# A chunked attention in one form for all blocks, with wide loads for the first six head pairs and W's first words ahead of block 1's loads

## The chip, the cores and the metric

The kernel runs on one core of one Trainium2 chip. The metric is the device time of one execution in microseconds. A core has TensorE (PE, with PEld for its weight loads), VectorE (DVE), ScalarE (ACT), GpSimd (POOL) and SyncE (SP). Loads and stores are issued from the queue of SP, POOL or ACT, and 16 DMA engines carry them.

## The reference

Three steps follow each other. First an attention in chunks: 4 batches, 8 heads, 768 tokens, heads of 64. A chunk of 32 tokens sees 16 tokens to its left, itself, 8 to its right, and 8 memory keys.

```python
for c in range(nc):
    l_start, r_end = max(0, c_start - left_ctx), min(S, c_end + right_ctx)
    k_full = np.concatenate([mem_k, k[:, :, l_start:r_end]], axis=2)
    v_full = np.concatenate([mem_v, v[:, :, l_start:r_end]], axis=2)
    scores = scale * np.matmul(q_c, k_full.transpose(0, 1, 3, 2))
    a = np.exp(scores - max); a = a / (sum(a) + 1e-09)
    out[:, :, c_start:c_end] = np.matmul(a, v_full)
```

Then two layers on the 3072 tokens by 512 columns: `g = h * tanh(softplus(h))` with `h = x @ w_in`, `x = g @ w_out` (hidden width 2048), and the same with `g = h * sigmoid(1.702 h)`. The four weights come as float64.

## The kernel before

The tokens go in 8 blocks (j) of 384. For each block the attention leaves x in a tile `xh` (and its low word in `xl`), and `forward(j, f)` multiplies it by 128 columns of w_in, for 16 f's (L1218). Block 0 does so in plain f32 (4 matmuls of 384 columns an f), blocks 1 to 7 as three products of a high and a low word (12 matmuls). Behind the first layer's forwards `across` and then `first` and `second` do the rest in products that are not touched here.

A float64 weight arrives as pairs of 32-bit words in `wi0` to `wi15`, and ACT and DVE make an f32 of it in `wo0` to `wo15` (`w_conv`: the drop L416 or L419, the shift L425, the low word L429, the sign L433). `split_words` then cuts it into two words for blocks 1 to 7 (L529, L534).

The attention stands in two forms. Blocks 0 and 1 use quads: the rows of all heads are loaded as they lie (`rows_of_heads`), turned on PE (`turned`, L761), multiplied four at a time (L829, L789), masked and reduced on DVE (`least`, L845), normed (L880), turned (L911, L991), multiplied with v (L928, L1013). Block 1's quads lie between block 0's forwards. Blocks 2 to 7 use duos of two head pairs: q and k are loaded in pieces of 32 columns (128 bytes), turned by DVE in 32 x 32 squares (L669, L672), the chunks' scores go to PE (L1054, 48 small matmuls, 96 instructions), then the maxima (L1069), exp (ACT, L1076), norm (L1088), three transposes a head (L1096), and the product with v (L1116, as many).

Every operation is handed to a planner (`Plan.add`) with a rank, costs for each engine that may do it, and the tiles that it reads and writes; `Plan.issue` writes each engine's order from these. The engines go through their own order one by one and wait where a tile isn't ready. A `Tag` is a set of buffers; the next user waits for the last one of the same buffer.

Of the kernel before, what the change touches and what calls it, by code (L numbers as in the profile page):

```python
# [9 lines left out]
F32 = mybir.dt.float32  # L10
# [8 lines left out]
EARLY = 2  # L19
WARM = 16  # L20
LEAD = 8
SOON = 12
AHEAD = 6
# [3 lines left out]
STAGGER = 1.5  # L27
LATE = 3
TURN = 2.7
# [70 lines left out]
class Spread:  # L100

    def __init__(self, before, *places):
        self.before, self.places, self.bufs = before, places, len(places)
        self.made = []
# [8 lines left out]
class Part:  # L113
# [9 lines left out]
    def __getitem__(self, key):  # L123
        return self.get()[key]

# [5 lines left out]
class Plan:  # L131
# [12 lines left out]
    def add(self, rank, ways, reads=(), writes=(), updates=(), chain=None, table=None):  # L144
# [5 lines left out]
        op.after, op.at = [], 0.0  # L150
        need = {}
# [7 lines left out]
        for b in (*writes, *updates):  # L159
# [3 lines left out]
            if not b.users and b.tag is not None:  # L163
                if b.inside is not None and b.inside.tag.made[0] is not b.inside:
                    below = b.inside.tag.made
                    k = below.index(b.inside)
                    b.gate += [(o, True) for o in below[k - b.inside.tag.bufs].users]
                    below[k - b.inside.tag.bufs].closed = True
                made = b.tag.made
                k = made.index(b)  # L170
                if isinstance(b.tag, Spread) and k < b.tag.bufs:
                    b.gate += [(o, True) for o in b.tag.before.get(b.inside, ())]
# [127 lines left out]
def bus(nbytes, run):  # L300
    return nbytes / 290e3 * (1 if run >= 512 else 1.3 if run >= 256 else 1.8)
# [3 lines left out]
def kernel(  # L305
# [24 lines left out]
    GQ = 96  # L330
    NG = S // GQ
    GB = TB // GQ
    WIN = P - NM
# [8 lines left out]
    NQ = H // 2 * (GB // 2)  # L342
    HV = H // 2
# [20 lines left out]
    T.update(ql=Shared(z0, 0), kl=Shared(z0, TB), mem_t=Shared(z0, TB + 32 * NKB), qT=Shared(z1, 0), kT=Shared(z1, 448))  # L364
    T.update(gh=Shared(z2, 0, TB), aT=Shared(z3, 0, TB))
    T.update(tags(ps, h=2, s0=1, s1=1, **{f"o{i}": 1 for i in range(4)}))
    for f in range(NF):
        T.update(tags(sb, **{f"{n}{f}": 1 for n in ("wi", "wo")}))

    def load(rank, buf, parts, nbytes, run, reads=(), early=False, via=None):  # L370

        for part in parts:
            def go(queue, part=part):
# [3 lines left out]
            size = bus(nbytes / len(parts), run)  # L377
            ways = [
                ("sp", 0.475, lambda go=go: go(nc.sync), size),
                ("pool", 1.2, lambda go=go: go(nc.gpsimd), size),  # L380
            ]
            add(rank, [("pool", 0.8, *ways[1][2:])] if via else ways if early else ways[:1], reads=reads, writes=[buf])
# [61 lines left out]
    def w_first(f):  # L444
        if f % 2 == 0:
            pairs.append(T[f"wo{f // 2}"].new([P, 2 * DM], F32))
# [1276 lines left out]
```

## Time and profile before

| | us |
|---|---|
| median of 3 runs (lowest, highest) | 1103.59 (1102.69, 1104.82) |
| the profiled execution | 1105.13 |
| its span | 1103.3 |
| busy in the span: PE, PEld | 1079.3, 1041.1 |
| busy in the span: DVE, ACT, POOL | 800.3, 555.8, 98.6 |

The profiled execution's own time is 1.8 us longer than its span, the part of the execution that lies around the profiled instructions. The shares of busy time are means over stages that are not alike: the start, in which loads and attention come first, block 0's forwards with block 1's attention between them, blocks 1 to 7, and the rest. The table of stretches below cuts there.

### The profile page before, as it was taken

How to read it: one execution, taken by the hardware profiler on the slowest of the kernel's cores; microseconds unless marked ns; L12 is line 12 of the kernel's file. 1: busy time of each engine (PE TensorE's matmuls, PEld its weight loads, DVE VectorE, ACT ScalarE, POOL GpSimd, SP SyncE). 2: the span in 40 equal slices, each digit the busy share in tenths (PEclk: the TensorE clock that was granted, in tenths of full speed). 3: DMA queues.
4: the chain of work that ended last, by engine and by line, in shares of the span. 5: the costliest groups of instructions: out<-in, count | busy, mean ns of one | idle time of the engine just before them, and what ended most of it. 6: DMA issues, size and time to landing. Idle time of an engine off the chain costs nothing.

```text
span 1103.3 us, 24808 instructions
## 1 busy us (share of the span) xinstructions
PE 1079.3 (98%) x9642; PEld 1041.1 (94%) x9642; DVE 800.3 (73%) x1456; ACT 555.8 (50%) x1246; POOL 98.6 (9%) x169
## 2 busy tenths in 40 slices
PE   7899999999999999999999999999999999999998
PEld 6568898989999999999999999999999999999998
DVE  5997656756556688899879856666657787877875
ACT  5875453545454455555455565555555533333332
POOL 2005642432300000000000000000000000000000
PEclk9999999999999999999999999999999999999999
DMA  9988998899986854663552686868688536345361
GB/s 172 264 241 189 242 247 228 205 250 268 278 276 222 249 175 147 216 212 121 189 172 86 208 260 223 296 227 290 203 265 261 160 106 166 112 133 145 105 165 46
DMA packets 278733, 221.28 MB, mean 201 GB/s; under 512 B 113553, under 2 KB 253868, under 8 KB 278616
## 3 DMA queue, kind: packets, MB, share of 16 engines
q1 hardware_dynamic: 272055, 209.46, 64.9%
q0 software_dynamic: 6560, 10.24, 3.8%
q8 instruction: 76, 1.25, 0.5%
q14 instruction: 42, 0.34, 0.1%
HBM read 138.33 MB, written 81.26 MB: 199 GB/s over the span
## 4 chain that ended last, share of the span: by engine, by line
PE 78%; DMA 10%; DVE 5%; SPq 4%; issue 1%; ACT 1%; DVEq 0%; ACTq 0%
PE o L1481 9%; PE o L1573 9%; PE h L1218 9%; PE o L1218 8%; PE h L1380 7%; PE o L1380 6%; PE s L1481 6%; PE h L1573 6%; PE h L1481 6%; PE s L1573 5%; SPq L375 4%; PE s L1380 3%; DMA st<-wd 3%; DMA st<-in_moe_w_out_dram 2%; DMA g1d<-ev 1%
## 5 line engine op out<-in xcount | busy, mean ns | idle before, releaser
L1218 PE MATMUL h<-xh,wi 128*128 128x384 f32 x320 | 82.9, 340 | 0.0
L1218 PE MATMUL o<-xh,wi 128*128 128x384 f32 x320 | 82.7, 339 | 0.0
L1218 PEld LDWEIGHTS h<-xh,wi 128*128 128x128 f32 x320 | 57.2, 188 | 0.6
L1218 PEld LDWEIGHTS o<-xh,wi 128*128 128x128 f32 x320 | 57.0, 188 | 0.5
L1218 PE MATMUL h<-xl,wi 128*128 128x384 f32 x160 | 53.7, 336 | 0.0
L1218 PE MATMUL o<-xl,wi 128*128 128x384 f32 x160 | 53.7, 336 | 0.0
L1350 ACT ACTIVATE e<-h 128x384 f32<-128x384 f32 (+2 forms) x47 | 22.4, 477 | 45.4 <-PE h L1573 28.8
L1573 PE MATMUL o<-wo,xh 128*128 128x256 f32 x232 | 43.7, 282 | 0.0
L1563 DVE TENSOR_TENSOR xl<-vt,xh 128x1024 fp32r<-128x1024 f32 x24 | 29.3, 1223 | 19.7 <-ACT xh L1560 18.0
L1563 DVE TENSOR_TENSOR xl<-wi,xh 128x1024 fp32r<-128x1024 f32 x32 | 38.8, 1222 | 5.9 <-ACT xh L1560 5.1
L1481 PE MATMUL o<-xh,wo 128*128 128x256 f32 x224 | 40.5, 282 | 0.0
L1560 ACT ACTIVATE xh<-wi 128x1024 fp32r<-128x1024 f32 x25 | 26.4, 1056 | 23.0 <-DMA wi<-gd 12.4
L375 POOL DMA_DIRECT2D vt<-in_v_dram x50 | 32.2, 648 | 63.3 <-PE o L1116 33.6
L375 POOL DMA_DIRECT2D wo<-in_v_dram x50 | 31.7, 638 | 53.7 <-PE o L1116 51.1
L1464 DVE TENSOR_TENSOR xl<-z,xh 128x1024 fp32r<-128x1024 f32 x24 | 29.2, 1222 | 9.7 <-ACT xh L1460 9.1
L1218 PE MATMUL o<-wo,wi 128*128 128x384 f32 x192 | 36.2, 340 | 0.0
L1573 PEld LDWEIGHTS o<-wo,xh 128*128 128x128 f32 x232 | 36.0, 190 | 0.0
L1218 PE MATMUL h<-wo,wi 128*128 128x384 f32 x192 | 35.7, 339 | 0.0
L1481 PEld LDWEIGHTS o<-xh,wo 128*128 128x128 f32 x224 | 34.6, 190 | 0.0
L1218 PEld LDWEIGHTS h<-wo,wi 128*128 128x128 f32 x192 | 33.2, 188 | 0.2
L1218 PEld LDWEIGHTS o<-wo,wi 128*128 128x128 f32 x192 | 33.0, 188 | 0.4
L1350 ACT ACTIVATE ev<-o 128x384 f32<-128x384 f32 (+2 forms) x31 | 14.5, 469 | 36.7 <-PE o L1573 17.5
(460 smaller groups left out, 3499.6 us busy)
## 6 DMA issues: line engine op xcount, KB each, us to landing
st<-in_moe_w_out_dram SPq DMA_DIRECT2D x32, 512.0 KB
st<-wd SPq DMA_DIRECT2D x29, 512.0 KB
z<-g1d SPq DMA_DIRECT2D x24, 512.0 KB
vt<-gd SPq DMA_DIRECT2D x24, 512.0 KB
wi<-gd SPq DMA_DIRECT2D x24, 512.0 KB
g1d<-gl SPq DMA_DIRECT2D x46, 192.0 KB
g1d<-z SPq DMA_DIRECT2D x45, 192.0 KB
wi<-in_moe_w_in_dram SPq DMA_DIRECT2D x16, 512.0 KB
```

What stands on the lines that cost most here:

```text
L375: queue.dma_start(out=o, in_=i)
L1218: nc.tensor.matmul(out=h.get(), lhsT=a[:, c], rhs=b.at(kk), start=(n == 0), stop=(n == KD * len(prods) - 1))
L1350: ("act", act(n, True), lambda: nc.scalar.activation(out=dst(), in_=bank.get(), func=AF.Copy)),
L1380: nc.tensor.matmul(out=bank.get(), lhsT=a, rhs=b, start=(fresh and m == 0), stop=(m == 3 * K2 - 1), skip_group_check=not fresh,)
L1464: add(rank + 0.05, [("dve", dve(n2), lambda gh=gh, gl=gl, src=src: nc.vector.tensor_tensor(out=flat(gl), in0=flat(src), in1=flat(gh), op=A ...
L1481: nc.tensor.matmul(out=bank[:, d, :], lhsT=a, rhs=b[:, p, :], start=(fresh and h == d == p == m == 0), stop=(h == 1 and p == HP - 1 and m ...
L1560: ("act", act(NP * P), lambda: nc.scalar.activation(out=flat(gh), in_=flat(src), func=AF.Copy)),
L1563: add(rank + 0.05, [("dve", dve(NP * P), lambda: nc.vector.tensor_tensor(out=flat(gl), in0=flat(src), in1=flat(gh), op=ALU.subtract))], re ...
L1573: nc.tensor.matmul(out=bank.get(), lhsT=a[:, p], rhs=b, start=(fresh and p == 0 and m == 0), stop=(p == NP - 1 and m == 2), skip_group_che ...
```

## The change

The quads go, with their masks, and all blocks use duos. `wide_pair` is new: for block 0's four head pairs and block 1's first two, q and k come in 1-KB pieces (4 tokens of a head in one partition), PE turns them by eight plain matmuls with the unit matrix (`turn`, L681), and ACT or DVE copies the result out in token order (L695, L696). The other pairs keep the 128-byte pieces. Block 0's q loads are issued by ACT; later blocks' q loads move from SP's queue to POOL's; all of v's come on POOL's. The memory rows of v are loaded for even blocks alone and stay in the tile for the odd ones. W's first words (for block 0) come in 2-KB pieces, two f's at a time and half of the 512 rows each, so that an f needs two tiles (`Joined`), and the ranks (LEAD is -2) place block 1's loads behind the first five of them. Block 0's h has three eviction buffers in place of two, and the planner's costs for a load (`bus`) are other ones.

The first forward in PE's order, before (L1218; `xh_312` is block 0's x, `wo0_469` the first W tile, `o1_551` and `ev_438` are block 0's scores and weights of a quad):

```order
L789 MATMUL o0_549<-z1_152 96x128
L789 MATMUL o1_551<-z1_152 96x128
L911 MATMUL o2_572<-ident_64,ev_438 128x96 x4
L928 MATMUL o3_585<-z3_267,vt_128 64x96 x4
L1218 MATMUL h_600<-xh_312,wo0_469 128x384 x4
L991 MATMUL s0_625<-ident_64,e_523 128x96 x4
L1218 MATMUL h_633<-xh_312,wo0_469 128x384 x4
L991 MATMUL s1_658<-ident_64,e_563 128x96 x4
L1218 MATMUL o2_663<-xh_312,wo1_544 128x384 x4
```

and after (L901 is the forward; `wo11_670` and `z1_80` are block 1's keys and queries of the second duo, `e_664` the weights of its first):

```order
L850 MATMUL s1_718<-z3_439,vt_315 64x32
L850 MATMUL o1_720<-z3_439,vt_315 64x32
L788 MATMUL s0_780<-wo11_670 32x64
L788 MATMUL o0_782<-wo11_670 32x64
L788 MATMUL s0_780<-z1_80 32x64
L788 MATMUL o0_782<-z1_80 32x64
L830 MATMUL s1_838<-ident_64,e_664 128x128 x3
L901 MATMUL h_845<-xh_635,wo0_313 128x384 x4
L901 MATMUL h_868<-xh_635,wo0_313 128x384 x4
L830 MATMUL o1_900<-ident_64,e_680 128x128 x3
L901 MATMUL o2_906<-xh_635,wo1_422 128x384 x4
L850 MATMUL s1_949<-z3_439,wo12_104 64x32
```

Before, the last product with v of block 0 (L928) stands just ahead of the first forward, and block 1's quads follow between the forwards. Now 48 scores matmuls of block 1's second duo and a group of transposes of its first stand ahead of it; rows that only repeat are left out.

DVE's order ahead of the first forward, before (`wo0_469` is a W tile in conversion, `e_563` and `mx_564` belong to block 1's quads):

```order
L918 COPY z3_267<-o2_513 128x384
L806 RECIPROCAL r_518<-r_518 96x4
L845 ISA e_523,mx_524<-s1_493,mask_70 96x128
L880 TENSOR_TENSOR ev_438<-ev_438,r_518 96x512
L965 COPY xh_312<-o3_539 128x192
L845 ISA e_563,mx_564<-s0_491,mask_70 96x128
L845 ISA e_563,mx_564<-s1_493,mask_70 96x128
L425 TENSOR_SCALAR wo0_469<-wo0_469 128x512
L425 TENSOR_SCALAR wo1_544<-wo1_544 128x512
```

and after (`z1_80` is the tile of queries and keys on which the scores above wait):

```order
L730 STREAM_TRANSPOSE wo11_670<-z0_194 128x384
L447 SCALAR_TENSOR_TENSOR wo2_488<-wi5_170,wo2_488 128x512
L733 STREAM_TRANSPOSE wo11_670<-z0_194 128x13x32
L730 STREAM_TRANSPOSE z1_80<-wo13_293 128x384
L646 COPY wo11_670<-z0_194 128x12x8
L433 TENSOR_SCALAR wo3_692<-wi6_323 128x512
L439 TENSOR_SCALAR wo3_692<-wo3_692 128x512
L555 TENSOR_TENSOR wi1_698<-wo0_313,wi0_515 128x512
L822 TENSOR_TENSOR e_680<-e_680,r_709 128x384
L733 STREAM_TRANSPOSE z1_80<-wo13_293 128x13x32
L443 SCALAR_TENSOR_TENSOR wo3_692<-wi6_323,wo3_692 128x512
L646 COPY z1_80<-z0_194 128x12x8
```

The maxima with mask (L845) are gone from there. W's conversion (L433, L439, L443, L447) now lies between the transposes of block 1's queries and keys (L730, L733), and the copy of the memory keys into `z1_80` (L646) closes them.

SP's queue at the start, after:

```order
L388 DMA wi12_92<-in_k_dram 100x2x256
L388 DMA wi13_96<-in_k_dram 100x2x256
L631 DMA wo12_104<-in_mem_k_dram 8x4x32 x4
L388 DMA wi14_98<-in_k_dram 100x2x256
L388 DMA wi15_102<-in_k_dram 100x2x256
L388 DMA wi0_136<-in_moe_w_in_dram 128x2x512
L388 DMA wi1_139<-in_moe_w_in_dram 128x2x512
L388 DMA wi2_142<-in_moe_w_in_dram 128x2x512
L388 DMA wi3_145<-in_moe_w_in_dram 128x2x512
L388 DMA wi4_155<-in_moe_w_in_dram 128x2x512
L388 DMA wi12_92<-in_q_dram 96x2x256
L388 DMA wi5_170<-in_moe_w_in_dram 128x2x512
```

k of block 0 comes first there, then five W tiles in 2-KB pieces (`128x2x512`), then block 1's first q; before, the queue began with block 0's k, q and v in pieces of 256 bytes.

```diff
@@ constants
-LEAD = 8
+FIRST = 4
+WIDE = 2
+LEAD = -2
@@ tags
+    T["ql"] = Spread((z0, 0), (w13, 0))
+    T["kl"] = Spread((z0, TB), (w13, TB))
+    T["qT"] = Spread(*((z, 0) for z in (z1, w15, w11)))
+    T["kT"] = Spread(*((z, TB) for z in (z1, w15, w11)))
+    T["vh"] = Spread(*((z, 0) for z in (w12, w14, *vs)))
...
@@ load
-            add(rank, [("pool", 0.8, *ways[1][2:])] if via else ways if early else ways[:1], reads=reads, writes=[buf])
+            way = ("sp", 0.475, lambda go=go: go(nc.sync), bus(nbytes / len(parts), run))
+            if on == "act":
+                way = ("act", 0.5, lambda go=go: go(nc.scalar), way[3])
+            elif via:
+                way = ("pool", via, lambda go=go: go(nc.gpsimd), bus(nbytes / len(parts), run, True))
...
@@ w_conv, w_first
+            k, c = (KD, 2 * P) if half is None else (KD // 2, 4 * P)
...
+        whole = T[f"wo{f // 2}"].new([P, 2 * DM], F32)
+        halves = [Part(whole, i * DM, DM) for i in range(2)]
+        for i in range(2):
+            w_conv(1, f, 0, f - 1.5, (), halves[i], f"wi{f + i}", i)
+            wi[f + i] = (Joined(halves, i),)
...
+    def wide_pair(j, hp, rank):
+        n, few = 4, LEFT // 4
+        nq, nk = TB // n, NKB * CHUNK // n
...
+        load(rank - lead, ql, [lambda: (
+            ql[:nq].rearrange("p h r d -> p h (r d)"), rows(q, r0, [(n, nq), (S, 2)], 0, n * D)
+        )], 2 * TB * D * 4, 1024, on=None if j else "act")
...
+        def turn(raw, m, t):
+            for r in range(n):
+                for hh in range(2):
+                    nc.tensor.matmul(
+                        out=t[hh * D:(hh + 1) * D, r * m:(r + 1) * m], lhsT=raw[:m, hh, r], rhs=ident[:m, :m],
+                        start=True, stop=True, tile_position=(0, hh * D),
+                    )
...
@@ pair_of_heads
+        if j == 0 or j == 1 and hp < WIDE:
+            return wide_pair(j, hp, rank)
...
-        load(rank - 4, ql, qs, P * TB * 4, 128)
-        load(rank - 4, kl, ks, P * NKB * 128, 128)
+        load(rank - (LEAD if j == 1 else 4), ql, qs, P * TB * 4, 128, via=NARROW * (j > 1))
+        load(rank - (LEAD if j == 1 else 4), kl, ks, P * NKB * 128, 128)
...
@@ values_of
+            if s0 == 0:
+                parts.append(lambda row=i * D + CHUNK, h=h: (
...
@@ forward
-        if j == 0:
-            w_cut(f)
-        t = T[("gh", "gl", "ev")[i % 3] if j else ("gh", "gl")[f % 2]].new([P, TB], F32)
+        if j == 0 and f % 2:
+            w_cut(f - 1)
+        t = T[("gh", "gl", "ev")[i % 3]].new([P, TB], F32)
```

## Rows read from the trace of the kernel before

**Rows 1.** Stretches of the span: start:end, length, busy us (instructions) of PE, PEld, DVE, ACT, POOL, clock, DMA, GB/s
```profile
0.00:39.07 39.07, 28.50 (x272) 23.67 (x272) 24.79 (x134) 24.71 (x99) 5.94 (x14) 0.96 1.01 201
39.07:94.20 55.13, 53.78 (x370) 33.40 (x369) 51.59 (x150) 39.51 (x124) 3.57 (x7) 1.00 0.88 230
94.20:380.00 285.80, 280.40 (x3634) 270.41 (x3633) 175.02 (x435) 139.39 (x468) 89.05 (x149) 1.00 0.89 245
```

**Rows 2.** Timeline of PE from 39 us: start us, us, engine, line
```profile
39.07 2.85 PE L1218 MATMUL h<-xh,wo 128*128 128x384 f32 x8
```

**Rows 3.** Stretches of 1 us at the start, columns as in rows 1
```profile
14.00:15.00 1.00, 0.00 (x0) 0.00 (x0) 1.00 (x11) 0.00 (x0) 0.00 (x0) 1.00 1.29 174
18.00:19.00 1.00, 1.00 (x8) 0.96 (x6) 0.00 (x0) 0.91 (x3) 0.00 (x0) 0.50 1.11 211
21.00:22.00 1.00, 1.00 (x12) 0.73 (x8) 1.00 (x7) 0.31 (x2) 0.00 (x0) 1.00 1.15 240
```

**Rows 4.** Chain of waits, 0 to 62 us: start us, us, what
```profile
45.57 5.19 PE o L1218 x16
50.76 0.41 PE h L761 x4
```

**Rows 5.** Groups of PE's instructions from 39.07 to 94.2 us
```profile
L991 PE MATMUL s<-ident,e 96*128 96x96 f32 x16 | 1.9, 249 | 0.2 <-DVE e L880 0.2
L1013 PE MATMUL s<-z,vt 128*64 128x96 f32 x32 | 1.8, 252 | 0.0
...
L761 PE MATMUL h<-ident,wi 96*128 96x96 f32 x8 | 1.7, 254 | 0.0
...
L789 PE MATMUL s<-u 64*96 64x128 f32 x16 | 1.1, 279 | 0.0
```

**Rows 6.** Chain of waits, 60 to 112 us
```profile
73.44 1.05 PE o L789 x16
...
86.71 0.66 PE o L991 x8
...
89.98 0.17 PE s L1054
...
91.08 0.81 PE o L1013 x16
...
99.27 0.48 PE o L1096 x3
...
108.09 0.17 PE s L1116
...
109.63 1.25 PE h L1218 x6
```

**Rows 7.** Timeline of DVE, 58 to 61 and 91.5 to 96 us
```profile
58.85 0.43 DVE L425 TENSOR_SCALAR wo<-wo 128x512 int32<-128x512 int32 x1 [0.36 <-ACT wo L416]
59.20 0.68 DVE L433 SCALAR_TENSOR_TENSOR wo<-wi,wo 128x512 int32<-128x512 int32 x1
59.80 0.68 DVE L429 SCALAR_TENSOR_TENSOR wo<-wi,wo 128x512 int32<-128x512 int32 x1
...
92.36 0.54 DVE L1069 TENSOR_REDUCE mx<-o 128x6 f32<-128x384 f32 x1
92.82 0.33 DVE L1071 TENSOR_SCALAR mx<-mx 128x6 f32<-128x6 f32 x1
92.88 0.60 DVE L672 STREAM_TRANSPOSE z<-wo 128x416 f32<-128x416 f32 x1
```

**Rows 8.** Timeline of PE at the start
```profile
1.36 6.67 PE L1631 MATMUL o<-ident 128*128 128x128 f32 x32 [1.36 <-POOL ident masks.py:199]
```

**Rows 9.** Waits of PE, 95 to 240 us: in total, times, longest
```profile
PE s L1096 <- DVE e L1088: 1.5, 1, 1.5
```

**Rows 10.** The page's costliest groups, POOL's loads of v
```profile
L375 POOL DMA_DIRECT2D vt<-in_v_dram x50 | 32.2, 648 | 63.3 <-PE o L1116 33.6
```

**Rows 11.** DMA issues: out<-in, queue, count, KB each, median us to landing
```profile
wi<-in_q_dram POOLq DMA_DIRECT2D x1, 192.0 KB, 8.9
```

## What the change is predicted to do

> **What bounds the kernel now.** I read the table of the stretches first, because the change acts on the start alone and a mean over the span hides it. The program's first matmul of the first layer (L1218, block 0) starts at 39.07 us [rows 2]; I call this moment T0. Before T0 PE works 28.50 of 39.07 us; behind it PE works 53.78 of 55.13 us, then 280.40 of 285.80, and DVE has room in both (51.59 of 55.13, 175.02 of 285.80) [rows 1]. The reader is to see two regimes: a start in which PE waits for others, and a rest in which PE is the bound. So the time is T0, plus the PE work that stands behind T0, plus the little PE idles there. The chain of waits says what a piece of that work takes: 16 matmuls of L1218 take 5.19 us, and 8 of them are one f of block 0 [rows 4], so block 0's sixteen take 8 x 5.19 = 41.5 us. The rest of the stretch 39.07 to 94.20 is block 1's attention, which lies between block 0's matmuls.
>
> The clock view shows a loss inside the start: PE does nothing from 14 to 15 us (it waits there for q and k), the clock is then granted at 0.50, and is at 1.00 again from 21 us [rows 3]. Half of the some 3.5 us between is lost, 1.75 us.
>
> **The change part by part.** *T0.* In the new order PE's first L901 is queued behind the scores of block 1's second duo, and their last operand is a key tile that DVE turns (L733) and completes (L646). So T0 hangs on DVE's order up to that copy. Counted there from block 0's first maxima: 13 W operations of the low and sign kind and 2 of the low-word kind at 0.60 us (59.20 to 59.80), 7 shifts and 2 drops at 0.35 (58.85 to 59.20), 21 operations of about 384 columns (6 maxima, 6 norms, 5 copies out of PSUM, 4 transposes) at 0.46 (92.36 to 92.82), 27 small ones at 0.1, where the one measured took 0.06 (92.82 to 92.88) [rows 7]. That is 9.0 + 3.15 + 9.7 + 2.7 = 24.5 us. It begins when block 0's first scores stand: the warm-up matmuls end at 8.03 [rows 8], six turnings (L681) behind them go in q, k pairs. A turning is 16 PE passes over 96 to 104 columns; the trace has none of it, so by its nearest rows: not under 0.41 us (L761's four, [rows 4]), not over 1.34 (L789's 1.05 for 16 of 128 columns [rows 6], with the quarter added that serial passes would cost); I take 0.85, near to L1013's 0.81 for 16 [rows 6]. 8.0 + 6 x 0.85 = 13.1, one duo's scores 1.1 (89.98 to 91.08 [rows 6]): 14.3. 14.3 + 24.5 + 0.6 for one stall at the first W word = 39.4; behind it half of the scores (0.6) and three transposes (0.48 [rows 6]). T0 = 40.5, 1.4 later than now. Ends: 37.5, where small operations go at 0.06 and ACT takes copies that I counted on DVE; 45, in the rival below.
>
> *What stands behind T0.* Before, block 1's attention still has there, by the groups of PE [rows 5] (each has a twin of the same count, o beside s, or wo beside wi) and their time in the chain: 32 of L991 at 0.66 for 8, 2.6; 64 of L1013 at 0.81 for 16, 3.2; 32 of L789 at 1.05 for 16, 2.1; 16 of L761 at 0.41 for 4, 1.6 [rows 4, 6]. Together 9.5 us. After, of block 1 there remain three transposes at 0.48 and two products with v at 1.54 (108.09 to 109.63 [rows 6]): 4.5. Saved: 5.0. The maxima with mask (L845) go from DVE and come back as plain maxima; both lie beside PE's work behind T0 and count nothing there. If DVE's room there were gone, its idle 3.5 us of that stretch [rows 1] would be the price.
>
> *Idle of that stretch.* 55.13 less 41.5, 9.5 and 1.1 (scores of block 2) is 3.0. It stems from PE pieces that wait for DVE or ACT between f's; with fewer pieces I keep half: -1.5. Bounds -3 and +1.5, by all of it going or half as much coming.
>
> *The clock at T0.* In the new order PE's work on attention before T0 lies in short pieces with waits for DVE, in the last of them some 5 us long. The only such wait in the trace, 13.7 to 17.2, is followed by 0.50 for some 3.5 us [rows 3]. I put one such dip at T0 and none at the start (block 0's q now comes from ACT's queue in 1-KB pieces, the warm-up runs straight into it): 1.75 now and inside T0, 1.75 then, partly behind T0. The one inside T0 is gone from the chain that I worked out afresh, so I charge +1.7. Bounds 0 and 6 (two more dips plus every small PE piece of the chain at half speed).
>
> The Trainium skill, "TensorE: Matmul & The Clock Gate", Part 1 on the HAM clock gate, says that the throttled state is the default and that activity releases it. The rows agree with the direction: 0.50 stands behind an idle stretch [rows 3]. It speaks against this change, whose start leaves PE sparse for longer; by it the clock would be low in the whole of 14 to 40 us, which is the first rival.
>
> *Queues.* Block 0's four q loads go to ACT, later blocks' q from SP to POOL. POOL's operation for v takes 0.648 us and the 50 of this group wait 63.3 us, most for PE's product [rows 10]; so a q load can stand behind a v load that waits. I cost it at -0.5 (SP is relieved of four issues a pair, odd blocks of eight memory loads). PE's longest wait between 95 and 240 us is 1.5 us [rows 9]; bounds -3 and +3, two of that size gone or come. The 2-KB pieces of W halve the number of pieces; W's tiles are not the last to come by the sum above, so that counts nothing; if they were, the price would be in T0 and within its bounds.
>
> *Sum:* +1.4 - 5.0 - 1.5 + 1.7 - 0.5 = -3.9. The profiled execution took 1105.13 us (span 1103.3 and 1.8 around it), 1.54 over the median 1103.59. 1105.13 - 3.9 = 1101.2, so a median of 1099.7 us. This case alone: 1096.5 to 1102.5, by the terms' bounds taken two at a time.
>
> **The rivals.**
> *A cold, late start.* From the first scores on PE is busy in pieces of 0.5 to 1.5 us with waits between; if 0.50 is granted all through, turnings, scores and transposes on the chain to T0 take twice as long: two more turnings and a scores group are 2 x 0.85 + 1.1 = 2.8 on it, and the copies wait with them. For: 18 to 21 us [rows 3]. Against: the mean clock of the whole start is 0.96 today, with PE at work in 28.50 of 39.07 us [rows 1]. T0 = 43.5 to 45, +3.5 on the sum: about 1103.3, no change.
> *More than forecast.* All idles of the stretch go, no dip, DVE's chain starts a turning earlier, T0 as now: -5.0 - 3.0 - 1 = -9, so about 1094.5. For: PE is the bound for the rest, and each us before it counts in full. Against: DVE's 24.5 us are in order.
> *Slower: POOL's queue holds q.* The stretch of blocks 1 to 7's first layer has two duos a block, one in 285.8 / 14 = 20.4 us [rows 1]. In a duo POOL issues 8 v and 8 q loads, 16 x 0.648 = 10.4 us; the v loads wait for the product of a duo before. What a q load then still needs is its landing and the DVE turning. The one q load of POOL in the trace took 8.9 us to land [rows 11]. 10.4 + 8.9 = 19.3, 1.1 under the period; with a landing over 10.0 us PE would wait. A landing 1 us over that would cost 1 us in each of the 12 duos of blocks 2 to 7: about 1111.7. For: 1.1 us is little. Against: that load moved 192.0 KB, and a q load of the new order moves 48 (32 partitions of 12 x 32 words).
> *It doesn't do what it says.* W's first words, issued earlier, might not land earlier, since W and block 0's loads share the DMA engines; T0 hangs on DVE's order all the same, so the sum stays, and its chance is part of the forecast's.
>
> **How the numbers follow.** Forecast 0.52, more than forecast 0.15, the cold start 0.20, POOL's queue 0.13. A measurement here can tell about 0.2% from no change, 1101.4 and 1105.8. Faster holds 0.40 of the forecast's 0.52, the 0.15, and 0.05 of the cold start: 0.60. Same holds 0.12 of the forecast and 0.12 of the cold start: 0.24. Slower: 0.03 of the cold start and all of POOL's: 0.16. The range 1093 to 1107 leaves out half of POOL's case and the end of "more": under 2 in 10.
>
> **What would show it.** T0 between 39.5 and 42 in the timeline of PE, with the scores of block 1's second duo just ahead of it; three L830 and two L850 groups of block 1 behind it; the first forward of block 1 some 49 us behind T0 (41.5 + 4.5 + 1.1 + 1.5 = 48.6, before 55.1). It is wrong if T0 is over 44, if the clock is at 0.50 behind 45 us, if PE waits between 95 and 380 us for keys or queries by more than 5 us in sum, or if PE's idles of block 0 stay at 3 us.

## The result and the profile after

The changed kernel takes 1112.51 us (median of 4 runs, 1112.08 to 1116.74), the kernel before 1103.38 beside it (4 runs, 1102.69 to 1104.82). The ratio is 1.009, interval 1.0063 to 1.0116. It is slower by 9.1 us; 3.9 less was predicted. The profiled execution took 1112.08 us. Ratios here and below are of fast executions; of all runs one execution, of e8_before_q_on_pool (3523.88 us), was slow.

The page after: busy us, share of the span and instructions, and the granted clock in 40 slices.

```profile
PE 1080.3 (97%) x10242; PEld 1046.0 (94%) x10242; DVE 790.4 (71%) x1342; ACT 536.1 (48%) x1183; POOL 167.5 (15%) x280
...
PEclk7699999999999999999999999999999999999999
```

PE is as busy as before (1080.3 against 1079.3), so 7 us more of span are not more work. The second and first slices show a lower clock.

The stretches after, columns as in [rows 1], cut at the first matmul of the first layer (T0), up to the first forward of block 1.

```profile
0.00:55.38 55.38, 35.19 (x816) 31.34 (x817) 30.22 (x86) 26.61 (x101) 25.29 (x48) 0.71 0.95 204
55.38:111.60 56.22, 53.26 (x625) 33.04 (x624) 42.11 (x104) 26.39 (x100) 38.10 (x62) 0.95 0.93 217
```

The line L901 of PE (count, shortest, median and longest ns, first and last start).

```profile
L901 PE MATMUL h<-xh,wi x320: 335/336/633, 111.6 to 380.8; 128*128 128x384 f32 x160
...
L901 PE MATMUL h<-xh,wo x64: 486/486/844, 55.4 to 102.8; 128*128 128x384 f32 x64
```

T0 is at 55.38 where it was at 39.07 [rows 1, 2]: +16.3. Block 1's forward starts at 111.6, before at 94.2. From T0 to there it is 56.2 us, 1.1 more than before. From there to the end it is 1110.3 - 111.6 = 998.7, before 1103.3 - 94.2 = 1009.1: -10.4. The sum is +7.0, the growth of the span. Behind the start the change gains 10 us; the start loses 17.

Waits of PE after, to 100 us: in total, times, longest.

```profile
PE h L681 <- DMA wi<-in_k_dram: 4.0, 2, 2.3
PE o L788 <- issue: 3.8, 1, 3.8
PE s L788 <- DVE wo L646: 3.8, 2, 2.4
PE s L788 <- issue: 3.7, 1, 3.7
PE h L681 <- DMA wi<-in_q_dram: 3.2, 1, 3.2
PE s L830 <- DVE mx L805: 2.2, 1, 2.2
```

There is no one wait: loads of q and k, DVE's copies and maxima, and two stops called issue share it. All are ahead of T0 but one of 2.4 us for a copy (L646). From 95 to 400 us PE waits for 0.6 us alone (before 5.5, of which [rows 9] is the longest).

DVE after, ahead of T0: start us, us, what, and in brackets its idle time and who ended it.

```profile
16.87 0.56 DVE L803 TENSOR_REDUCE mx<-s 128x6 f32<-128x384 f32 x1
...
19.29 0.43 DVE L439 TENSOR_SCALAR wo<-wo 128x512 int32<-128x512 int32 x1 [1.20 <-ACT wo L430]
...
25.10 0.13 DVE L802 MEMSET o<- 32x32 f32 x2 [3.53 <-PE o L788]
...
32.86 0.56 DVE L696 COPY z<-h 128x384 f32<-128x384 f32 x1 [2.62 <-PE h L681]
...
39.69 0.59 DVE L696 COPY wo<-h 128x416 f32<-128x416 f32 x1 [1.82 <-PE h L681]
...
51.35 0.60 DVE L733 STREAM_TRANSPOSE z<-wo 128x416 f32<-128x416 f32 x1
```

The last copy ahead of the scores (L646) runs from 52.45 to 52.64. Of the 35.8 us from the first maxima to there, eight idles take 11.0 and the work 24.8.

The clock after, in stretches with columns as in [rows 1]:

```profile
14.00:18.00 4.00, 4.00 (x128) 3.58 (x126) 1.25 (x6) 0.52 (x1) 1.45 (x3) 0.50 1.07 262
...
22.00:26.00 4.00, 0.43 (x5) 0.19 (x4) 0.90 (x5) 2.22 (x13) 1.62 (x4) 0.64 1.08 272
26.00:42.00 16.00, 9.93 (x162) 8.74 (x164) 10.52 (x29) 8.51 (x33) 1.54 (x5) 0.50 0.88 157
42.00:44.00 2.00, 2.00 (x114) 1.83 (x110) 1.17 (x3) 0.77 (x2) 1.35 (x3) 0.60 0.95 257
...
52.00:56.00 4.00, 2.82 (x95) 2.36 (x95) 3.45 (x8) 0.95 (x2) 0.67 (x3) 0.50 1.06 205
```

From 14 to 18 us, behind PE's wait for block 0's last k, the clock is at its lower level, 1.2 GHz. PE works 0.43 of the 4 us from 22, then the clock is there again for 16 us in which PE works 9.93, and once more around T0. The mean over the start is 0.71, before 0.96 [rows 1].

SP's queue after (DMAs issued, start and length of the stretch of issues):

```profile
9.48 3.86 SPq L388 DMA_DIRECT2D wi<-in_moe_w_in_dram  x5
...
17.11 2.04 SPq L388 DMA_DIRECT2D wi<-in_q_dram  x1
...
37.78 2.03 SPq L388 DMA_DIRECT2D wo<-in_q_dram  x4
```

The chain of waits has one long piece there, block 1's second q:

```profile
17.11 18.49 DMA wi<-in_q_dram
```

It is issued behind the six W tiles (3.1 MB) and takes 18.49 us to 35.6. The DMA engines are busy for 0.95 of the start and move 204 GB/s; before they were as full (1.01, 201 GB/s [rows 1]) with less to bring ahead of T0.

### The profile page after: what moved, and what is told of

The parts are those of the page before. It is cut to its first block, busy times and chain, and to the rows that moved or that the text cites. A ratio compares the mean times of both kernels' runs of the same rounds, so it can differ in the third digit from the quotient of the medians.

```text
span 1110.3 us, 25866 instructions
## 1 busy us (share of the span) xinstructions
PE 1080.3 (97%) x10242; PEld 1046.0 (94%) x10242; DVE 790.4 (71%) x1342; ACT 536.1 (48%) x1183; POOL 167.5 (15%) x280
## 4 chain that ended last, share of the span: by engine, by line
PE 87%; DMA 9%; DVE 2%; SPq 1%; issue 1%; ACT 1%; ACTq 0%; DVEq 0%
PE o L901 12%; PE h L901 12%; PE o L1164 9%; PE o L1256 9%; PE h L1063 7%; PE o L1063 6%; PE h L1256 6%; PE h L1164 6%; PE s L1164 6%; PE s L1256 6%; PE s L1063 3%; DMA st<-wd 3%; DMA wi<-in_q_dram 2%; PE s L850 1%; DMA z<-in_k_dram 1%; DMA wo<-in_mem_k_dram 1%
## 5 line engine op out<-in xcount | busy, mean ns | idle before, releaser
L901 PE MATMUL h<-xh,wi 128*128 128x384 f32 x320 | 83.3, 342 | 0.0
L901 PE MATMUL o<-xh,wi 128*128 128x384 f32 x320 | 83.1, 341 | 0.0
L901 PEld LDWEIGHTS o<-xh,wi 128*128 128x128 f32 x320 | 57.1, 188 | 0.5
L901 PEld LDWEIGHTS h<-xh,wi 128*128 128x128 f32 x320 | 57.1, 188 | 0.5
L901 PE MATMUL o<-xl,wi 128*128 128x384 f32 x160 | 54.0, 337 | 0.0
L901 PE MATMUL h<-xl,wi 128*128 128x384 f32 x160 | 53.9, 337 | 0.0
L388 POOL DMA_DIRECT2D wo<-in_v_dram x66 | 42.2, 645 | 44.2 <-PE o L850 38.3
L388 POOL DMA_DIRECT2D vt<-in_v_dram x66 | 42.1, 644 | 35.4 <-PE o L850 29.4
L1147 DVE TENSOR_TENSOR xl<-z,xh 128x1024 fp32r<-128x1024 f32 x24 | 29.3, 1224 | 16.2 <-ACT xh L1143 14.9
L1164 PE MATMUL o<-xh,wo 128*128 128x256 f32 x224 | 40.5, 282 | 0.0
L810 ACT ACTIVATE e<-s,mx 128x64 f32<-128x64 f32 x90 | 26.9, 320 | 19.1 <-DVE mx L805 17.0
L901 PE MATMUL h<-wo,wi 128*128 128x384 f32 x192 | 36.0, 340 | 0.0
L901 PE MATMUL o<-wo,wi 128*128 128x384 f32 x192 | 35.5, 340 | 0.0
L901 PEld LDWEIGHTS o<-wo,wi 128*128 128x128 f32 x192 | 33.0, 188 | 0.4
```

What stands on the lines that cost most here:

```text
L388: queue.dma_start(out=o, in_=i)
L810: nc.scalar.activation(out=e[:, g, i], in_=s[hh][:, g, i], func=AF.Exp, scale=scale, bias=mx[:, g, i:i + 1], accum_out=sm[:, g, i:i + 1],)
L901: nc.tensor.matmul(out=h.get(), lhsT=a[kk], rhs=b.at(kk), start=(n == 0), stop=(n == KD * len(prods) - 1))
L1147: add(rank + 0.05, [("dve", dve(n2), lambda gh=gh, gl=gl, src=src: nc.vector.tensor_tensor(out=flat(gl), in0=flat(src), in1=flat(gh), op=A ...
L1164: nc.tensor.matmul(out=bank[:, d, :], lhsT=a, rhs=b[:, p, :], start=(fresh and h == d == p == m == 0), stop=(h == 1 and p == HP - 1 and m ...
```

## The experiments

The theories at the start were four: the order of the loads (W in front of block 1's), the clock, PE's supply of instructions, and block 1's work that stands ahead of the first layer in queues that go in order. The bytes through the DMA engines came later as a fifth. All runs were timed over three rounds beside the kernel before. T0 and the start of block 1's forward come from the profile of each. A ratio is to the kernel before of the same session.

### Parts undone

**e1_loads_first.** Block 1's loads go ahead of W's, 1-KB pieces kept.

```diff
-LEAD = -2
+LEAD = 8
```

> Block 1's loads of q and k are put ahead of W's third and later tiles again (the constant LEAD from -2 to 8); all else as in the changed kernel. Theory Q (the first forward is late because block 1's loads stand behind five W tiles in SP's queue, and PE meets block 1's turnings ahead of block 0's products with v): the turnings that waited until 31.3 and 35.3 us wait no more than to about 24, T0 falls from 55.4 to 43 to 49, the time from 1112.5 to 1101 to 1107. Theory C (the half clock from 14 to 44 us makes the start late): T0 stays within 3 us of 55.4, the time over 1109. Theory F (duos in the first blocks are slow as such, whatever comes first): W's words are late in their place, T0 stays over 52, the time over 1109.

Measured: 1108.68, ratio 1.0039 (1.002 to 1.0058); T0 55.6, block 1's forward 107.7. T0 does not move, what follows it is 4 us shorter (52.1 against 56.2).

**e16_pieces_undone.** Block 1 wholly in 128-byte pieces turned by DVE, W first.

```diff
-WIDE = 2
+WIDE = 0
```

> The part of the change on block 1's pieces undone alone (WIDE 0): its first two pairs come in 128-byte pieces too and are turned by VectorE, so that TensorE has no turnings of block 1. The order then puts the first layer behind one duo of block 1 (two groups of scores, two of its transposes) instead of two. Theory in-order queues (each piece of block 1's work that stands ahead of the first layer costs its hand-overs and TensorE's stops for instructions): 64 turnings and one duo less, first matmul of the first layer at 45 to 50, waits called issue 4 us or less, time 1103 to 1109. Rival landing (128-byte pieces land late): first matmul at 53 or later, with waits for q or k in front of it, time 1110 to 1117.

Measured: 1113.65, 1.0075 (1.0055 to 1.0096); T0 54.2, forward 112.5. The expected 45 to 50 is missed though a duo's scores and 64 matmuls of turnings less stand ahead of T0: how much stands ahead is not enough to set it. PE's stops called issue take 12.4 us there (6.2, 5.1 and two of 1.1 together), where 4 or less were expected.

**e17_both_undone.** `WIDE = 0` and `LEAD = 8` together.

```diff
-WIDE = 2
-LEAD = -2
+WIDE = 0
+LEAD = 8
```

> Both named parts undone (WIDE 0, LEAD 8): block 1's loads stand ahead of W's first tiles, in 128-byte pieces. It goes with e16_pieces_undone and tells what W's place counts without the wide pieces. Theory in-order queues: W lands behind the narrow loads, so that the first layer waits for W's words; first matmul at 46 to 52, time 1104 to 1110. Rival landing: the loads ahead land sooner, first matmul at 42 to 46, time 1100 to 1105.

Measured: 1105.02, 1.0006 (0.9983 to 1.0028); T0 46.4, forward 103.2. The whole loss is gone. The two last kernels run the same number of PE's instructions in each stretch, up to T0 in the same order but for one group of scores, so their rows can be laid side by side. With W first (e16), the stretches up to T0, to block 1's forward and to the end:

```profile
0.00:54.20 54.20, 29.14 (x656) 25.46 (x657) 30.17 (x83) 27.46 (x103) 25.34 (x48) 0.63 0.92 207
54.20:112.50 58.30, 55.78 (x720) 34.81 (x720) 41.94 (x104) 27.81 (x102) 41.06 (x68) 0.93 0.90 221
112.50:1109.40 996.90, 991.84 (x8806) 982.20 (x8804) 716.89 (x1151) 484.13 (x986) 99.73 (x163) 1.00 0.65 198
```

With block 1's loads first (e17):

```profile
0.00:46.40 46.40, 27.63 (x656) 24.56 (x657) 24.73 (x74) 23.81 (x96) 23.07 (x45) 0.69 0.96 202
46.40:103.20 56.80, 53.65 (x720) 33.70 (x720) 47.95 (x116) 29.46 (x106) 38.39 (x64) 0.98 0.98 244
103.20:1099.20 996.00, 990.62 (x8806) 981.25 (x8804) 717.60 (x1153) 482.41 (x983) 104.68 (x172) 1.00 0.65 199
```

Of 10.2 us, 7.8 lie ahead of T0, where PE has 656 matmuls in both: its idle is 54.20 - 29.14 = 25.1 against 18.8, and the lower clock makes the same work 1.5 longer. 1.5 lie in the second stretch, 0.9 behind it. SP's queue tells how block 1's first loads differ. W first (e16):

```profile
9.31 2.21 SPq L388 DMA_DIRECT2D wi<-in_moe_w_in_dram  x4
11.56 10.11 SPq L388 DMA_DIRECT2D z<-in_q_dram  x4
21.72 6.28 SPq L388 DMA_DIRECT2D z<-in_k_dram  x4
...
30.64 2.25 SPq L388 DMA_DIRECT2D wo<-in_k_dram  x4
```

Block 1's loads first (e17):

```profile
8.55 3.31 SPq L388 DMA_DIRECT2D z<-in_q_dram  x4
11.91 3.20 SPq L388 DMA_DIRECT2D z<-in_k_dram  x4
...
18.51 2.38 SPq L388 DMA_DIRECT2D wo<-in_k_dram  x4
20.93 3.65 SPq L388 DMA_DIRECT2D wi<-in_moe_w_in_dram  x6
```

Four W tiles ahead make the same 16 issues end at 32.9 and not at 20.9: behind 2 MB of W, an issue of q that takes 0.8 us takes 2.5.

But ahead of T0 the engines hardly wait for these loads: DVE 0.6 us in e16, and more, 3.7 us, in e17. What differs in PE's idle is its stops called issue, 12.4 us against 3.5. W first (e16):

```profile
PE s L788 <- issue: 6.2, 1, 6.2
PE o L850 <- issue: 5.1, 1, 5.1
```

Block 1's loads first (e17):

```profile
PE s L850 <- issue: 3.5, 1, 3.5
```

The stop of 6.2 stands in block 0's own scores, so block 0's first maxima start at 22.11 us in e16 and at 15.82 in e17:

```profile
22.11 0.56 DVE L803 TENSOR_REDUCE mx<-s 128x6 f32<-128x384 f32 x1
...
15.82 0.56 DVE L803 TENSOR_REDUCE mx<-s 128x6 f32<-128x384 f32 x1
```

That is 6.3 of the 7.8 us, before any engine waits for a load of block 1. The packet of instructions that ends this stop lands at 20.14 us, the same packet of e17 at 10.96 (last section). The last wait ahead of T0 in e16 is for W itself: ACT evicts block 0's x (L861) at 52.95, behind two conversions (L430) that waited 2.3 and 0.8 us for W tiles. Each reading is of one profile, and no run changes when these packets land and nothing else.

**e3_all_wide.** The other way: all of block 1 in 1-KB pieces.

```diff
-WIDE = 2
+WIDE = 4
```

> All four pairs of block 1 come in 1-KB pieces and are turned on PE (WIDE from 2 to 4): 16 issues of 128-byte pieces become 4 in SP's queue. Q: the second duo's operands land some 8 us earlier, T0 at 46 to 51, the time 1104 to 1109, though PE has four turnings more (0.85 to 1.7 us each). C and F: no gain from it, T0 at 55 or later, the time 1111 to 1116.

Measured: 1120.26, 1.0139 (1.0119 to 1.0159); T0 63.1, forward 118.5. More pieces turned on PE, a later T0. PE's stops called issue take 14.2 us ahead of it, in the changed kernel 7.5 (3.8 and 3.7).

### Which wait sets T0

**e2_block1_later.** Block 1's ranks eight later.

```diff
-        base = ... 4 if j == 1 else SOON
+        base = ... -4 if j == 1 else SOON
```

> Block 1's attention gets ranks eight f's later, so that the first forward stands ahead of the scores of its second duo and behind those of its first; the loads keep W's first tiles ahead. Q: the narrow loads of the second duo no longer hold T0, which then hangs on the wide ones alone: T0 at 45 to 50, the time 1104 to 1109. C: T0 over 52. F: T0 falls as with Q, but block 1's forward comes no earlier than 110 us, since the work is only moved behind T0; the time over 1110.

Measured: 1117.06, 1.0106 (1.0076 to 1.0137); T0 54.5, forward 108.1, but its second f starts only at 121.2: block 1's work comes too late behind T0, and ranks alone do not bring T0 forward.

**e4_warm_pe.** Six plain matmuls ahead of each scores group of blocks 0 and 1 and of block 1's turned queries.

```diff
+            for _ in range(6 if j < 2 else 0):
+                nc.tensor.matmul(out=s[0]..., lhsT=ident.get(), rhs=ident.get(), start=True, stop=True)
```

> Six matmuls of the unit matrix with itself, whose results are written over, stand ahead of the scores of blocks 0 and 1 and ahead of block 1's turnings of q, where PE waits 2 to 4 us. C: the clock is granted at 1.00 for most of 20 to 44 us, T0 falls by 4 us or more, the time to 1108 or less. Q and F: the clock rises, but the waits for loads end when they did, T0 stays within 2 us of 55.4, the time within 3 of 1112.5.

Measured: 1114.7, 1.0087 (1.006 to 1.0113); T0 58.2, forward 112.6. Columns as in [rows 1]:

```profile
38.00:44.00 6.00, 6.00 (x240) 5.60 (x236) 4.45 (x12) 3.58 (x7) 2.89 (x5) 1.00 0.77 175
```

From 38 to 44 the clock is full where it was 0.50 to 0.60, and nothing is won. But the 72 matmuls on the unit matrix are 13.0 us of PE's work ahead of T0 themselves. So the run shows that the clock brought up in this way doesn't pay, not that the low clock costs nothing.

**e5_shifted_stream.** Sixteen matmuls of two columns behind the warm-up, to move PE's stops called issue.

```diff
+        for _ in range(16):
+            nc.tensor.matmul(out=spare[:, :2], lhsT=ident.get(), rhs=ident[:, :2], start=True, stop=True)
```

> The changed kernel with 16 small matmuls of two columns behind the warm-up, whose result nothing reads: they move every later PE instruction 64 places down (each counts for two matmuls and two weight loads) and cost about 1 us while PE waits for k anyway. Theory I (PE runs out of its instruction stream at fixed counts, behind its 347th and 721st matmul in two kernels of different order, and waits 2 to 4 us for the next piece): the stops come 32 matmuls earlier in the program, out of the second duo's scores or shorter; PE's waits with no releaser within 20 to 54 us fall from 7.5 us by 3 or more or stand at other lines, and T0 falls by 2 to 6 us, the time to 1107 to 1111. Theory D (the stops are waits for late loads or a full bus at 21 and 50 us): they stand before the same matmuls as before, T0 within 1.5 us of 55.4.

Measured: 1108.76, 1.0046 (1.0029 to 1.0063); T0 54.6, forward 111.0. The stops stay at the same counts (last section), so they fall on another operation. Ahead of T0 they take 7.6 us for 7.5, and T0 is 0.8 earlier. The ratio is 0.4% under the changed kernel's, with intervals that touch at 1.0063; where that comes from was not traced.

**e6_landing.** The planner reckons 8.0 us for a landing.

```diff
-LANDING = 3.5
+LANDING = 8.0
```

> The planner's allowance from a load's issue to its landing goes from 3.5 to 8 us for the early ranks; the order of PE then has block 0's products with v ahead of block 1's turnings. Theory O (PE's order follows loads that the planner takes to be early, and so blocks on block 1's q and k at 31.3 and 35.3 us): T0 falls by 4 to 10 us, the time to 1103 to 1109. Theory S (T0 hangs on the sum of DVE's work and PE's stops, whatever stands first, since block 1's scores still stand ahead of the first forward): T0 stays within 3 us, the time over 1109.

Measured: 1110.53, 1.0061 (1.0039 to 1.0082); T0 54.2, forward 110.3. The planner's view of the landings moves T0 by 1.2 us: it is not the cause.

**e14_two_tiles, e15_four_tiles.** Fewer of W's tiles ahead of block 1, so fewer bytes ahead of T0.

```diff
-AHEAD = 6
+AHEAD = 2    # e15: 4
```

> The changed kernel with two of W's tiles ahead instead of six (AHEAD 2), so that four tiles of 512 KB stand behind block 1's loads. Theory bytes (the DMA engines are busy for 0.95 of the first 55 us at 203 GB/s, and the first layer starts when what stands ahead has landed): 2.1 MB less ahead of it, at 203 GB/s 10.3 us, first matmul of the first layer at 44 to 48. Rival in-order queues (the copies, maxima and turnings of block 1 that stand ahead on VectorE and TensorE, and TensorE's stops for its instructions, set it whatever lands): 53 to 57. Either way W's third and later tiles come late behind it, so that the time falls by less than the first matmul: by bytes forward of block 1 from 106 to 112 and 1106 to 1113, by the rival 110 to 118 and 1112 to 1120.

> As e14_two_tiles with four of W's tiles ahead (AHEAD 4), the dose between. Theory bytes: 1.05 MB less ahead, 5.2 us, first matmul of the first layer at 49 to 52. Rival in-order queues: 53 to 57. Time 1106 to 1113 by bytes, 1111 to 1116 by the rival.

Measured: e14 1119.64, 1.013 (1.0106 to 1.0153), T0 52.9, forward 116.6; e15 1113.36, 1.008 (1.0056 to 1.0104), T0 58.6, forward 111.2. The theory of bytes falls for T0 (44 to 48 and 49 to 52 expected). The chain of e14 says why:

```profile
15.43 10.14 DMA wi<-in_k_dram
...
36.12 2.22 issue
...
41.75 3.56 ACT e L810 x24
...
47.44 1.42 issue
```

DVE copies the last of block 1's keys that PE turned at 32.14 us, in the changed kernel at 39.69. Of these 7.5 us T0 gains 2.5: stops of PE, ACT's exps and DVE's transposes take the place of the landing.

### Block 1 behind the first layer

**e9_block1_behind.** Block 1's turnings and scores wait for the first forward's first value; its ranks are two later.

```diff
-            if f == 0 and j + 1 < NB:
+            if f == (j == 0) and j + 1 < NB:
...
-        add(r0 + SCORE, [("pe", COSTS, scores)], reads=reads, writes=s)
+        add(r0 + SCORE, [("pe", COSTS, scores)], reads=reads + ([pace[0]] if j == 1 else []), writes=s)
...
-        base = ... 4 if j == 1 else SOON
+        base = ... 2 if j == 1 else SOON
```

> The changed kernel with one dependence more: block 1's turnings and scores wait in the planner for the first forward (attention of block 1 is added behind it), so that on PE, DVE and ACT block 0's own work stands ahead; the loads keep their ranks. Theory B (T0 is late because block 1's two duos stand ahead of block 0's last steps in the in-order queues, wait there for loads and hold PE at half clock): T0 falls from 55.4 to 37 to 43, and the time to 1092 to 1102. Theory I+D (PE's stops for its instruction stream, the clock and the loads of block 0 itself set T0): T0 at 48 or later, the time 1106 or more.

Measured: 1114.12, 1.0074 (1.0047 to 1.0101); T0 41.1, forward 111.0. T0 comes 14.3 us sooner: what made it late is block 1's work in front of it in the engines' queues. But the 14 us are lost again. The waits from 36 to 125 us:

```profile
PE h L901 <- ACT xh L861: 5.3, 1, 5.3
...
ACT wo L430 <- DMA wi<-in_moe_w_in_dram: 10.8, 3, 6.6
```

ACT stands at L430 for W tiles that are not there; the evictions that the forwards need (L861) are queued behind. SP issued none of W from 13.6 to 38.98 us, in which block 1's 128-byte loads are.

**e10_behind_and_13, e11_behind_loads_first.** As e9, with `WARM` 16 to 13, and with `LEAD` -2 to 8.

```diff
-WARM = 16
+WARM = 13     # e10
-LEAD = -2
+LEAD = 8      # e11
```

> As e9, with 13 warm-up matmuls in place of 16, that is 12 instructions fewer ahead of the second duo's scores of block 0. Theory I (PE stops for the next piece of its instruction stream at a fixed count, behind its 347th matmul, within those scores): the scores end before that count, their maxima start 2 to 4 us earlier, T0 falls by 2 to 4 against e9. Without I: T0 as in e9 within 1 us.

> As e9, with block 1's loads ahead of W's fifth and later tiles (LEAD 8). Theory B alone: T0 within 2 of e9's, since nothing of block 1 stands ahead of it, and the time within 3 of e9's. Theory Q (the place of the loads against W counts by itself): the waits of block 0's forwards for block 1's q and k go, the time 3 to 6 under e9's; if W's later tiles are then late, 3 or more above.

Measured: e10 1114.07, 1.0071 (1.0048 to 1.0095), T0 40.0, forward 113.7; the stop in block 0's second duo (4.4 us in e9) is gone, and PE's wait for DVE's maxima there grows from 2.2 to 4.4 us (L805). e11 1117.26, 1.0098 (1.0068 to 1.0128), T0 39.7, forward 117.3, with 13.2 us at L901 for ACT.

**e12_behind_ahead_10, e13_behind_ahead_16.** As e9, and W's tiles may go 10 or 16 ahead.

```diff
-AHEAD = 6
+AHEAD = 10    # e13: 16
```

> Block 1's scores and turnings wait for the forward's first value, as in e9_block1_behind (first matmul of the first layer at 41.1 us, forward of block 1 from 111.0, 25 us of waits for W's tiles by the traced sums of ScalarE and VectorE), and W's tiles may be issued ten ahead of the layer that uses them instead of six, so that SP issues W6 to W9 among block 1's first loads and not behind them. Theory SP's order (the narrow loads of block 1 stand in one in-order queue ahead of W's tiles, and the engines of the DMAs have room for both): waits for W's tiles together 3 us or less, forward of block 1 from 104 or earlier, time 1104 or less. Rival bytes (the engines of the DMAs carry about 210 GB/s here, and block 1's pieces and W's tiles are late by their sum): forward of block 1 still from 107 to 112, time 1109 to 1116, with the waits moved from W's tiles to block 1's q and k. Either: first matmul 39 to 43.

> As e12_behind_ahead_10, with W's tiles sixteen ahead: all of the first forward's tiles stand ahead of most of block 1's loads. Theory SP's order: no wait for W's tiles, and the narrow loads of block 1, now last, hold its scores: forward of block 1 from 100 to 106, time 1101 to 1107. Rival bytes: forward of block 1 from 107 to 113 again, waits all on block 1's q and k, time 1109 to 1117.

Measured: e12 1122.82, 1.0173 (1.014 to 1.0205), T0 47.4, forward 123.3; e13 1122.23, 1.0175 (1.0152 to 1.0198), T0 47.0, forward 123.1. Both theories had less. Waits of e12, 36 to 125 us:

```profile
PE h L901 <- ACT xh L861: 11.6, 1, 11.6
PE s L830 <- ACT xh L861: 7.5, 1, 7.5
...
ACT wo L430 <- DMA wi<-in_moe_w_in_dram: 13.6, 7, 2.5
```

With more of W ahead the planner puts more of W's conversion ahead too, and ACT's queue waits for it in front of the evictions of block 0 itself.

**e18_behind_pieces_undone.** As e9 with `WIDE` 0.

```diff
-WIDE = 2
+WIDE = 0
```

> As e9_block1_behind (block 1's scores wait for the first layer's first value), with block 1's first two pairs in 128-byte pieces, so without its 64 turnings on TensorE. First matmul of the first layer 39 to 42 by every theory. If W's tiles that landed late in e9 (forward of block 1 from 111.0) were late behind the pieces of block 1 in SP's queue, they are as late here: forward of block 1 from 107 to 113, time 1109 to 1116. If the turnings and their hand-overs made it late: from 98 to 104, time 1102 to 1108.

Measured: 1115.35, 1.0098 (1.0069 to 1.0127); T0 40.4, forward 114.2. As late as e9, without a turning of block 1 on PE: W behind block 1's loads, not the turnings, holds the forwards there (PE waits 13.5 us at L901 for an eviction).

### POOL's queue for q

**e7_q_on_sp.** The queries of blocks 2 to 7 back on SP.

```diff
-        load(..., ql, qs, P * TB * 4, 128, via=NARROW * (j > 1))
+        load(..., ql, qs, P * TB * 4, 128, via=0)
```

> The changed kernel with the q loads of blocks 2 to 7 issued from SP's queue again. If the move to POOL took PE's waits behind the first forward of block 1 away (5.4 us of idle before, 0.5 after), they come back: the time rises by 3 to 6, to 1115 to 1118. If other parts did it (the order, the memory rows of v, the buffers), the time stays within 2 of 1112.5.

Measured: 1124.78, 1.0192 (1.0175 to 1.0208); T0 54.3, forward 110.1. From 100 to 390 us PE waits again, 7.8 of the 9.2 us here:

```profile
PE s L830 <- DVE e L822: 7.8, 3, 4.0
```

**e8_before_q_on_pool.** The kernel before with its queries of blocks 2 to 7 from POOL.

```diff
-        load(rank - 4, ql, qs, P * TB * 4, 128)
+        load(rank - 4, ql, qs, P * TB * 4, 128, via="pool")
```

> The kernel before with one edit: the q loads of blocks 2 to 7 (and the pairs that it loads in 128-byte pieces) go through POOL's queue. If the queue was the cause of the waits behind 95 us, the time falls by 3 to 5, to 1098 to 1101; if not, within 2 of 1103.4. If POOL's queue holds q behind v loads that wait, it rises to 1107 or more.

Measured: 1101.7, 0.9987 (0.9969 to 1.0005); T0 39.8, forward 94.7: no change that can be told from none. The changed kernel needs POOL for q, the one before does not.

The Trainium skill, "DMA: Bandwidth & Descriptors", Issuing engine by pattern, sends simple loads to SP and calls the hardware queues generally faster than GpSimd's. Here the same loads from SP cost 1.0192 - 1.009, about 1%. The Trainium skill, same page, Issuing engines are not separate DMA queues, says that another issuer only saves the sequencer's time. That this time is what SP lacks is not shown by a run here.

## Why the prediction was wrong

**T0, the step that failed.** It said that T0 hangs on DVE's order, with 0.6 us for one stall. DVE's work was sized right (24.5; measured 24.8). Its idles were not: 11.0 for 0.6. The chain began at 16.87 and not at 14.3 (14.2 by its own terms), since block 0's last k landed at 13.35 and its turning ran at the lower clock (1.66 for 0.85). The tail from the last copy to T0 took 2.7 for 1.1. 10.4 + 0.3 + 2.6 + 1.6 = 14.9, the whole distance from 40.5 to 55.38. The count took DVE for always supplied. By what ended them, the eight idles are 3.5 for a stop of PE for instructions (at 24.6 us), 4.4 for turnings of block 1 (PE had waited 3.2 for the first q and 1.7 for a k), 1.2 for ACT's conversion of W, and 1.9 for others.

**PE's stops for instructions.** The prediction has no term for them. Ahead of T0 they take 7.5 us in the changed kernel; the kernel before has none there.

**"W's tiles are not the last to come, so that counts nothing."** This is the part of it that the experiments size. Putting W ahead costs 1.0075 against 1.0006 with 128-byte pieces (e16, e17), and 1.009 against 1.0039 with 1-KB ones (after, e1): 0.7% and 0.5%, 8 and 6 us. In both pairs block 1's loads come later behind W, but the loss is not simply a wait for them. With 1-KB pieces T0 stays with the loads first; the gain lies behind T0, where PE idles 0.3 us and not 3.0. With 128-byte pieces T0 falls by 7.8, most of it from PE's stops, and a W tile is late after all (e16). That W in front delays the instructions is thus read from one pair and not shown in general: in the changed kernel, with W in front too, the first packet lands at 12.95 us, and PE doesn't stop there. The 1-KB pieces of block 1 cost 0.33% with the loads first (e1, e17) and 0.15% with W first, which can't be told from nothing; in both the intervals overlap. With both undone nothing of the 9 us is left (e17).

**What was added in front.** That block 1's scores stand ahead of the first forward was seen, and its price was not: with them behind it T0 is 41.1 (e9). That this is nearly the predicted 40.5 is chance, since 40.5 was summed with them in front. But no kernel that put them behind was faster, as W then comes late.

**The clock.** One dip of 1.7 us was charged, at T0, and none at the start. The clock is low from 14 to 18 us, for 16 us from 26, and again from 52 to 56. So two of the four signs named for a wrong forecast came true, T0 over 44 and 0.50 behind 45 us; a third, idles of block 0 that stay at 3 us, did too (below). The rival of a cold start foresaw the low clock and put T0 at 43.5 to 45. Its mechanism is there: a turning of k takes 0.93 us at the full clock (e4) for the 1.66 here, so the 9.93 us of work from 26 to 42 would be some 5.6, an estimate. What of that would reach T0 is open, since e4 brought the clock back only by work of its own. The Trainium skill, "TensorE: Matmul & The Clock Gate", Part 1, has the low clock as the default state that activity lifts. The row at 26 us agrees, with 9.93 us of work in 16.

**What stands behind T0.** Three L830 and two L850 groups and one of scores were foreseen, 48.6 us in all. There are five, three and two: one product with v, one group of scores and two of transposes more, 1.54 + 1.1 + 2 x 0.48 = 3.6 us of work of block 2, which is then missing behind block 1's forward. The first 16 matmuls take 6.26 us at the lower clock for 5.19 [rows 4], 1.1 more, and PE's idle is 56.22 - 53.26 = 3.0 for the 1.5 kept (2.4 of it the wait for the copy at L646, 0.6 a stop). That makes 54.8 of the 56.2; the rest lies in further dips of the clock. So most of this saving was not lost: it lies in the -10.4, with the 5.4 of the next point; 1.4 of it were not traced.

**Idle and queues.** -1.5 and -0.5 were charged for idles and queues behind T0. The 3.0 of idle that the first halves was a remainder of a sum; by [rows 1] PE idles 55.13 - 53.78 = 1.35 there, less than the 1.5 that was to go. From block 1's forward to the end of block 7's PE idled for 5.4 us before (94.2 to 380) and now for none (111.6 to 390), so -5.4; POOL's queue for q takes part in that (e7). The rival that POOL's queue holds q is refuted: PE waits for no q from 95 to 400 us. DVE waits once, 5.2 us to 119.6, and PE doesn't feel it. That the rival's 1111.7 us is near the measured 1112.5 is chance.

**What stays open.** Which of the hand-overs makes T0 55 and not 46 in the changed kernel can't be named alone: warmth, landing allowance, place of the stops, bytes ahead each moved T0 by 3.2 us or less (e4, e6, e5, e14, e15), and in e14 another wait is seen to take the place of the one removed. Laid beside e17, the 9.0 us by which T0 is later are 7.6 of PE's busy time (816 matmuls for 656) and 1.4 of idle. Also why e17, with T0 7 us later than before, is no slower: its last stretch is 996.0 us against 1009.1, of which waits and block 2's early work were read in the changed kernel, not in e17.

## What to carry to other kernels

When a start is full of DMA and every engine takes its instructions in order, a sum of one engine's work up to a point is a lower bound, not a forecast: add a wait for each hand-over between engines, the landing of what is queued in front, and PE's stops at its counts of instructions. Bytes over the rate alone did not forecast T0 (e14, e15). Work of a later stage moved into such a start should be costed with its loads, and a load that "isn't the last to come" still makes those behind it later. When no single removal helps, undo the parts in pairs: the four kernels e16, e17, e1 and after told what single edits had not.

## What the runs showed of the hardware

PE stops at fixed counts of its instructions. In the changed kernel it stands from 21.0 to 24.7 us in the middle of a scores group:

```profile
0.00:21.00 21.00, 17.18 (x347) 15.92 (x348) 5.70 (x19) 6.76 (x17) 13.46 (x28) 0.84 0.91 200
21.00:24.70 3.70, 0.10 (x3) 0.09 (x4) 0.57 (x1) 3.22 (x20) 2.30 (x4) 0.79 1.07 279
```

With 64 instructions more ahead of it (e5) the stop stands behind the same counts, on other operations:

```profile
0.00:21.50 21.50, 18.86 (x347) 18.07 (x348) 5.01 (x17) 6.32 (x15) 13.71 (x28) 0.92 0.93 201
```

This is position 706 in PE's program. Further stops come at 450, 962, 1218 and 1474, so always 256 apart, and a 16-KB packet of the instruction queue lands about 1.5 us before PE goes on (after: 22.07 to 23.21, PE at 24.61). With the DMA engines full the long ones took 2 to 6.2 us (e16's at 450). In the kernel before, 272 matmuls stand ahead of T0 where 816 do after, so there are fewer such counts in the start, and PE doesn't stop at the one that is there (450). So many small matmuls can have a price that their busy time doesn't show.
